# A two-layer GELU block on one core: the last wait of the program moves from SyncE to GpSimd

## The chip, the core and the metric

The kernel runs on one core of a Trainium2 chip. The metric is the device time of one execution in microseconds (us). A core has five engines with instruction streams of their own: TensorE (PE, matrix multiplication; its weight loads are listed as PEld), VectorE (DVE), ScalarE (ACT), GpSimd (POOL) and SyncE (SP), which only issues transfers and waits. The engines meet through semaphores alone: an instruction or a transfer raises one when it is done, and another engine waits until it has a given value. A transfer raises its semaphore by 16 when all of its data has landed.

## The reference

```python
B, S, D, F = 1, 2048, 448, 1792          # bfloat16 throughout

def reference(x, w1, b1, w2, b2):
    h = jnp.einsum("bsd,df->bsf", x, w1) + b1
    h = _gelu(h)                          # the tanh approximation
    return jnp.einsum("bsf,fd->bsd", h, w2) + b2
```

## The kernel before

**Tiles and stages.** The 2048 tokens are worked on in four chunks of 512 (`NSC`), the 1792 hidden features in fourteen tiles of 128 (`NFT`). TensorE first turns the first chunk of x with matmuls against an identity matrix (`turn_x`); the other three chunks come in turned by the transfers. The first layer (`l1`, matmuls at L275) runs over all pairs of chunk and feature tile, in an order that is written out by hand for the opening, while the weights are still arriving. ScalarE applies bias and GELU to each finished PSUM bank (L380) and writes `g_sb`. The second layer (`l2`, matmuls at L354) goes over the sixteen token tiles of 128, fourteen matmuls each. VectorE adds the second bias (L408) and writes `out_sb`.

**Outputs.** The list `outs` has seventeen entries: fifteen token tiles of 448 columns, and the last token tile cut in two, 320 columns and 128 columns. VectorE raises `sem_osb` by one after each. Every store is made by the helper `store` (L173) and raises `sem_od` by 16 when it has landed.

**Who issues and who waits.** SP (`sync_work`, from L217) issues nearly all loads and then the first sixteen stores, each behind a wait for its `sem_osb`. ScalarE (`scalar_work`) issues two loads at its start and the last store, of 128 columns, at its end. GpSimd (`gpsimd_work`) builds the identity matrix (a memset at L235 and an affine_select at L237), issues one small load (L242) that fills up rows of `b1n_sb`, and ends. The last instruction of `sync_work`, at L232, is the wait for all seventeen stores: `sem_od` at 16 x 17 = 272. No other engine waits for `sem_od`. At the start of the program all five engines pass a barrier (listed at L432), in which GpSimd gathers the others and releases them.

Of the kernel before, what the change touches and what calls it, by code (L numbers as in the profile page):

```python
# [11 lines left out]
def bass_standalone__dense_activation_gelu__prompt_kernel(  # L12
# [105 lines left out]
    outs = [(j, 0, D) for j in range(NST - 1)] + [(NST - 1, 0, OCUT), (NST - 1, OCUT, D)]  # L118
# [6 lines left out]
    with ExitStack() as es:  # L125
# [38 lines left out]
        sem_od = S_("sem_od")  # L164
# [5 lines left out]
        def store(eng, n):  # L170
            j, c0, c1 = outs[n]
            to = out0_view[:, j, c0:c1] if j < STC else out2[j * P:(j + 1) * P, c0:c1]
            eng.dma_start(to, out_sb[:, j, c0:c1]).then_inc(sem_od, 16)  # L173
# [7 lines left out]
        def load_w1p(eng, k, i):  # L181
            a, b = W1_PIECES[i]
            r = KROW[k]
            with nc.allow_non_contiguous_dma(reason="w1 column pieces"):
                eng.dma_start(
                    w1_sb[:, k, a * P:b * P], w1[r:r + P, a * P:b * P]
                ).then_inc(sem_w1p[k][i], 16)

        def load_w1(eng):
            with nc.allow_non_contiguous_dma(reason="w1 column pieces"):  # L190
                for k in (3, 2):
                    n, r = ROWS[k], KROW[k]
                    eng.dma_start(w1_sb[0:n, k, 0:WCUT], w1[r:r + n, 0:WCUT]).then_inc(sem_w1[k], 16)
                eng.dma_start(w1_sb[:, 3, WCUT:F], w1[KROW[3]:D, WCUT:F]).then_inc(sem_w13, 16)
                eng.dma_start(
                    w1_sb[:, 0:2, WCUT:F], w1[0:2 * P, WCUT:F].rearrange("(k p) f -> p k f", p=P)
                ).then_inc(sem_w1r, 16)
                eng.dma_start(
                    w1_sb[0:HALF, 2, WCUT:F], w1[KROW[2]:KROW[2] + HALF, WCUT:F]
                ).then_inc(sem_w1r, 16)  # L200

        def load_w2(eng, i):
            a, b = W2_PIECES[i]
            eng.dma_start(
                w2_sb[:, a:b, :], w2[a * P:b * P, :].rearrange("(ft p) d -> p ft d", p=P)
            ).then_inc(sem_w2[i], 16)

        def load_xT(eng, c):
            for k, d0 in enumerate(KROW):
                eng.dma_start(  # L210
                    xT_sb[:, k, c * SC:(c + 1) * SC],
                    x2[c * SC:(c + 1) * SC, d0:d0 + P],
                    transpose=True,
                ).then_inc(sem_x[c], 16)

        def sync_work(sp):
            sp.dma_start(xn_sb[:, 0:2, :], x0_view[:, 0:2, :]).then_inc(sem_xn[0], 16)  # L217
            sp.dma_start(xn_sb[:, 2:4, :], x0_view[:, 2:4, :]).then_inc(sem_xn[1], 16)
            load_w1p(sp, 0, 1)
            for i in range(len(W1_PIECES)):  # L220
                load_w1p(sp, 1, i)
            load_w1(sp)
            load_xT(sp, 1)
            for c in range(2, NSC):
                load_xT(sp, c)
            for i in range(len(W2_PIECES)):
                load_w2(sp, i)
            sp.dma_start(b2_bc[:, :], b2.partition_broadcast(P)).then_inc(sem_b2, 16)
            for n in range(len(outs) - 1):
                sp.wait_ge(sem_osb, n + 1)  # L230
                store(sp, n)
            sp.wait_ge(sem_od, 16 * len(outs))  # L232

        def gpsimd_work(pool):
            pool.memset(ident[:, :], 0.0).then_inc(sem_id, 1)  # L235
            pool.wait_ge(sem_id, 1)
            pool.affine_select(  # L237
                out=ident[:, :], in_=ident[:, :], compare_op=ALU.not_equal, fill=1.0,
                base=0, pattern=[[-1, P]], channel_multiplier=1,
            ).then_inc(sem_id, 1)  # L240

            pool.dma_start(b1n_sb[NFT:SQ, :], w1[0:SQ - NFT, 0:P]).then_inc(sem_b1x, 16)  # L242

        def tensor_work(pe):
            ones_w = nc.const_aps.tensor(1.0, [P, P], BF16)
# [166 lines left out]


        sync_work(nc.sync)
        gpsimd_work(nc.gpsimd)
        tensor_work(nc.tensor)
        scalar_work(nc.scalar)
# [29 lines left out]
```

## Time and profile before

| what | value |
|---|---|
| median of three runs | 93.5 us (93.33 to 93.71) |
| the profiled execution | 93.2 us |
| its span, from the program's first instruction to the end of its last | 91.9 us |
| granted TensorE clock, mean over the span | 1.00 |
| TensorE busy | 89.2 us |
| ScalarE busy | 36.6 us |
| VectorE busy | 12.8 us |
| GpSimd busy | 1.3 us, 7 instructions |
| stores, from issue to landing | 1.5 to 2.6 us, median 1.7 us |

The span holds only the program's own instructions. The execution's time is longer than the span by what lies before the first and after the last of them, and the trace has no row for that part. Semaphore instructions and the issue of transfers are not counted as busy; they stand in the rows of the queues (SPq, ACTq, POOLq). "L173" is line 173 of the kernel; a line of a helper such as `store` collects the instructions of all who call it.

### The profile page before, as it was taken

How to read it: one execution, taken by the hardware profiler on the slowest of the kernel's cores; microseconds unless marked ns; L12 is line 12 of the kernel's file. 1: busy time of each engine (PE TensorE's matmuls, PEld its weight loads, DVE VectorE, ACT ScalarE, POOL GpSimd, SP SyncE). 2: the span in 40 equal slices, each digit the busy share in tenths (PEclk: the TensorE clock that was granted, in tenths of full speed). 3: DMA queues.
4: the chain of work that ended last, by engine and by line, in shares of the span. 5: the costliest groups of instructions: out<-in, count | busy, mean ns of one | idle time of the engine just before them, and what ended most of it. 6: DMA issues, size and time to landing. Idle time of an engine off the chain costs nothing.

```text
span 91.9 us, 1491 instructions
## 1 busy us (share of the span) xinstructions
PE 89.2 (97%) x650; PEld 47.3 (52%) x650; DVE 12.8 (14%) x27; ACT 36.6 (40%) x61; POOL 1.3 (1%) x7
## 2 busy tenths in 40 slices
PE   6999999999999999999999999999999999999991
PEld 4664445555555555555545555555555555555571
DVE  0172000000000000000000122222112222221141
ACT  2640999877977788778974000000000000000000
POOL 5000000000000000000000000000000000000000
PEclk9999999999999999999999999999999999999999
DMA  1999856445795000000000111011111100111111
GB/s 26 342 303 274 143 112 85 95 101 114 199 375 182 0 0 4 7 0 0 0 0 0 50 55 47 7 48 50 50 50 50 50 28 29 50 50 50 50 50 50
DMA packets 12594, 7.29 MB, mean 79 GB/s; under 512 B 7203, under 2 KB 12396, under 8 KB 12588
## 3 DMA queue, kind: packets, MB, share of 16 engines
q1 hardware_dynamic: 12240, 7.03, 29.1%
q10 hardware_dynamic: 316, 0.17, 0.6%
q8 instruction: 5, 0.08, 0.3%
q0 software_dynamic: 32, 0.00, 0.0%
q14 instruction: 1, 0.01, 0.0%
HBM read 3.79 MB, written 1.84 MB: 61 GB/s over the span
## 4 chain that ended last, share of the span: by engine, by line
PE 97%; DVE 0%; issue 0%
PE ps L275 46%; PE ps L354 46%; PE ps L248 3%; PE ps L258 2%; DVE out_sb L408 0%
## 5 line engine op out<-in xcount | busy, mean ns | idle before, releaser
L275 PE MATMUL ps<-xT_sb,wi_sb 64*128 64x512 bf16 (+2 forms) x384 | 42.8, 374 | 0.0
L354 PE MATMUL ps<-wo_sb,g_sb 128*128 128x448 bf16 (+2 forms) x238 | 42.6, 342 | 0.0
L380 ACT ACTIVATE g_sb<-ps,bi_f 128x512 bf16<-128x512 f32 x56 | 33.7, 694 | 9.5 <-PE ps L275 9.5
L354 PEld LDWEIGHTS ps<-wo_sb,g_sb 128*128 128x128 bf16 x238 | 22.7, 98 | 20.2 <-issue 0.4
L275 PEld LDWEIGHTS ps<-xT_sb,wi_sb 64*128 64x128 bf16 (+1 forms) x384 | 21.8, 94 | 20.4 <-issue 0.7
L408 DVE TENSOR_TENSOR out_sb<-ps,bo_bc 128x448 bf16<-128x448 f32 (+2 forms) x17 | 10.2, 597 | 71.2 <-PE ps L354 71.2
L248 PE MATMUL ps<-const-bfloat16-1.0 128*128 128x256 bf16 x12 | 2.7, 417 | 0.8 <-PEq L432 0.8
L248 PEld LDWEIGHTS ps<-const-bfloat16-1.0 128*128 128x128 bf16 x12 | 1.6, 143 | 1.4 <-issue 0.8
L372 ACT ACT_TABLE_LOAD x1 | 1.3, 1283 | 1.8 <-issue 1.8
L376 ACT CAST xT_sb<-ps 128x512 bf16<-128x512 f32 (+1 forms) x3 | 1.5, 514 | 1.3 <-PE ps L258 1.3
L391 DVE CAST xT_sb<-ps 128x256 bf16<-128x256 f32 x3 | 1.2, 422 | 4.2 <-PE ps L258 4.2
L258 PE MATMUL ps<-ident,xn_sb 128*128 128x128 bf16 x16 | 1.6, 251 | 0.0
L258 PEld LDWEIGHTS ps<-ident,xn_sb 128*128 128x128 bf16 x16 | 1.3, 116 | 0.6 <-issue 0.5
L404 DVE COPY wi_sb<-wi_sb 64x512 bf16<-64x512 bf16 (+1 forms) x2 | 0.6, 286 | 2.0 <-DMA wi_sb<-in_w_dram 2.0
L396 DVE STREAM_TRANSPOSE bit_sb<-bin_sb 32x32 bf16<-32x32 bf16 x4 | 0.8, 200 | 0.1
L242 POOL DMA_DIRECT2D bin_sb<-in_w_dram x1 | 0.7, 655 | 0.2 <-issue 0.2
L237 POOL TENSOR_SCALAR_AFFINE_SELECT ident<-ident 128x128 bf16<-128x128 bf16 x1 | 0.3, 287 | 0.2 <-POOL ident L235 0.2
L372 ACT ACTIVATE act_junk<-const-float32-0.0 128x8 bf16<-128x8 f32 x1 | 0.2, 208 | 0.0
L235 POOL MEMSET ident<- 128x128 bf16 x1 | 0.2, 204 | 0.3 <-POOLq L432 0.3
L398 DVE CAST bi_f<-bit_sb 128x14 f32<-128x14 bf16 x1 | 0.2, 175 | 0.0
L432 POOL MEMSET const-float32-0.0<- 128x1 f32 x1 | 0.1, 98 | 0.2 <-issue 0.2
L432 POOL MEMSET const-bfloat16-1.0<- 128x1 bf16 x1 | 0.1, 101 | 0.0
(2 smaller groups left out, 0.2 us busy)
## 6 DMA issues: line engine op xcount, KB each, us to landing
out_dram<-out_sb SPq DMA_DIRECT2D x15, 112.0 KB, 1.7
wo_sb<-in_w_dram SPq DMA_DIRECT2D x2, 784.0 KB, 5.5
wi_sb<-in_w_dram SPq DMA_DIRECT2D x4, 128.0 KB, 3.5
xn_sb<-in_x_dram SPq DMA_DIRECT2D x2, 224.0 KB, 2.8
wi_sb<-in_w_dram SPq DMA_DIRECT2D x1, 384.0 KB, 5.1
wi_sb<-in_w_dram SPq DMA_DIRECT2D x1, 256.0 KB, 4.0
wi_sb<-in_w_dram SPq DMA_DIRECT2D x1, 192.0 KB, 4.5
xT_sb<-in_x_dram SPq DMA_TRANSPOSE x12, 3.4
```

What stands on the lines that cost most here:

```text
L242: pool.dma_start(b1n_sb[NFT:SQ, :], w1[0:SQ - NFT, 0:P]).then_inc(sem_b1x, 16)
L248: pe.matmul(ps[0][:, 0:WN], lhsT=ones_w, rhs=ones_x, start=True, stop=True)
L258: mm = pe.matmul(ps[XBANK[n]][:, col:col + P], lhsT=xn_sb[:, 2 * h + t, KROW[k]:KROW[k] + P], rhs=ident[:, :], start=True, stop=True,)
L275: return pe.matmul(bank("g", i)[:, t0:t1], lhsT=w1_sb[lo:hi, k, ft * P:(ft + 1) * P], rhs=xT_sb[lo:hi, k, c * SC + t0:c * SC + t1], start= ...
L354: mm = pe.matmul(bank("o", n)[:, 0:c1 - c0], lhsT=g_sb[:, ft, j * P:(j + 1) * P], rhs=w2_sb[:, ft, c0:c1], start=(ft == 0), stop=(ft == NF ...
L372: act.activation(act_junk[:, :], zero, ACT.Gelu_apprx_tanh)
L376: act.copy(*x_part(n, parts)).then_inc(sem_xTa, 1)
L380: act.activation(g_sb[:, ft, c * SC:(c + 1) * SC], bank("g", i)[:, :], ACT.Gelu_apprx_tanh, bias=b1_f[:, ft:ft + 1], scale=1.0,).then_inc( ...
L391: dve.tensor_copy(*x_part(n, parts)).then_inc(sem_xTd, 1)
L396: dve.transpose(b1t_sb[to, :], b1n_sb[:, to]).then_inc(sem_b1T, 1)
L404: dve.tensor_copy(two(HALF, 2), two(0, 3)).then_inc(sem_dup, 1)
L408: dve.tensor_tensor(out=out_sb[:, j, c0:c1], in0=bank("o", n)[:, 0:c1 - c0], in1=b2_bc[:, c0:c1], op=ALU.add,).then_inc(sem_osb, 1)
```

## The change

The wait for all stores is taken out of SP's stream and put at the end of GpSimd's. SP's last instruction is then its sixteenth store; GpSimd's last instruction is the wait. The semaphore and the count are the same.

```diff
@@ -229,7 +229,6 @@
             for n in range(len(outs) - 1):
                 sp.wait_ge(sem_osb, n + 1)
                 store(sp, n)
-            sp.wait_ge(sem_od, 16 * len(outs))
 
         def gpsimd_work(pool):
             pool.memset(ident[:, :], 0.0).then_inc(sem_id, 1)
@@ -240,6 +239,7 @@
             ).then_inc(sem_id, 1)
 
             pool.dma_start(b1n_sb[NFT:SQ, :], w1[0:SQ - NFT, 0:P]).then_inc(sem_b1x, 16)
+            pool.wait_ge(sem_od, 16 * len(outs))
 
         def tensor_work(pe):
```

## The prediction, made before the changed kernel had run

> **What bounds the kernel now.** I read the page's busy times first, then the chain that ended last in order of time, then the timeline of the last microseconds, then what SP's queue waited for, and last the start of the program, because it is the only place where GpSimd (POOL) and SP do the same thing side by side.
>
> The head of the page and its busy times:
>
> ```profile
> span 91.9 us, 1491 instructions
> PE 89.2 (97%) x650; PEld 47.3 (52%) x650; DVE 12.8 (14%) x27; ACT 36.6 (40%) x61; POOL 1.3 (1%) x7
> ```
>
> TensorE is busy for 89.2 of 91.9 us; GpSimd runs seven instructions. The chain that ended last (start us, length us, what):
>
> ```profile
> 5.48 42.02 PE ps L275 x380
> 47.49 42.53 PE ps L354 x238
> 90.02 0.02 issue
> 90.05 0.29 DVE out_sb L408
> ```
>
> The chain is TensorE from 0.8 to 90.0 us and one VectorE addition. It stops at 90.34 us (90.05 + 0.29), because the chain follows work and not transfers; the span ends 1.56 us later. The timeline from 85 us on shows what fills that:
>
> ```profile
> 89.26 0.49 DVE L408 TENSOR_TENSOR out_sb<-ps,bo_bc 128x320 bf16<-128x320 f32 x1 [1.28 <-PE ps L354]
> 90.05 0.29 DVE L408 TENSOR_TENSOR out_sb<-ps,bo_bc 128x128 bf16<-128x128 f32 x1 [0.29 <-PE ps L354]
> 90.37 0.35 ACTq L173 DMA_DIRECT2D out_dram<-out_sb  x1
> ```
>
> ScalarE's queue issues the last store at 90.37 us, 0.03 us after the addition. The DMA part of the page gives 1.5 us from that issue to landing, so it lands at about 91.87 us. SP's queue waits for it:
>
> ```profile
> SPq L173 <- DVE out_sb L408: 60.8, 16, 27.3
> SPq L232 <- DMA out_dram<-out_sb: 1.7, 1, 1.7
> L232 SPq EVENT_SEMAPHORE  x1: 17/17/17, 91.9 to 91.9; - x1
> ```
>
> The first two lines are SP's waits (us in total, times, longest); the third is the record of line 232 (duration in ns, then its start). SP is done with its sixteen stores at 90.1 us, waits 1.7 us, and its wait record of 17 ns closes the span. So the tail is: last addition, ScalarE's issue, landing, and whoever stands at that wait.
>
> **The change, part by part.** The profiled execution took 93.2 us, which is its span of 91.9 us and 1.3 us that lie outside the program's own instructions. The median of the three runs is 93.5 us, so I add 0.3 us to any sum made against the profiled execution.
>
> *Removed:* one 17 ns record on SP at 91.875 us (91.892 less 0.017). SP then ends with the store of outs[15]; its issue starts at 89.78 us by the trace and lasts 0.33 us, so SP ends at 90.1 us. Nothing stands behind line 232 on SP, and nothing waits for it.
>
> *Added:* one wait on POOL for the same semaphore with the same count, 16 x 17 = 272. It opens with the same landing at 91.87 us. POOL's records of this kind, at the start of the program, have the same length as SP's:
>
> ```profile
> L432 POOLq EVENT_SEMAPHORE  x2: 17/17/17, 0.5 to 0.6; - x2
> L432 SPq DRAIN  x1: 7/7/7, 0.0 to 0.0; - x1
> L432 POOLq DRAIN  x1: 193/193/193, 0.3 to 0.3; - x1
> L432 SPq EVENT_SEMAPHORE  x1: 17/17/17, 0.7 to 0.7; - x1
> ```
>
> 17 ns against 17 ns: the exchange of the record itself is worth 0.00 us. In program order the wait stands after POOL's memset, its affine_select and its one DMA issue (L242, 1.66 to 2.32 us), so none of them moves, and nothing is queued behind it. From 2.32 us on POOL has no work in either version, and nobody waits for POOL after the identity and the b1x load are there. The wait passes no issue on POOL's queue, and SP's queue issues the same 16 stores at the same times. The cover of all this is POOL's idleness; if POOL had to issue anything after 2.32 us, that issue would stand behind the wait until 91.87 us, but there is no such instruction. TensorE's 89.2 us, the last addition and ScalarE's issue are untouched, so the landing at 91.87 us stays.
>
> *How late POOL notices.* No row shows POOL waiting for a DMA. From below: when POOL and SP leave the opening barrier together, POOL's first instruction starts at 0.74 us and SP's first issue at 0.75 us, so POOL is no slower at leaving a wait, within 0.01 us. From above: between POOL's memset (ends 0.94 us) and the affine_select that waits for its semaphore (starts 1.18 us) lie 0.23 us, against 0.03 us between VectorE's addition and ScalarE's issue. That larger figure includes the end of the memset's writes and a register instruction, which a bare wait does not have. So 0.0 to +0.2 us; I take 0.0, because the barrier row is a sequencer's wait as this one is.
>
> *What follows the last wait.* The 1.3 us outside the span is the only part of the time that is large enough to matter, and the trace has no instruction in it. How it divides between the front and the end is not shown. If all of it is what SP has to do after its last instruction, and POOL needs nothing, the change gains 1.3 us. If POOL needs twice as long as SP, as its DMA issue does (655 ns at L242 against 332 ns for SP's stores), the change loses 1.3 us. So -1.3 to +1.3 us. The nearest rows are again at the start: the engines' first records begin at 0.0 us for SP, 0.1 us for VectorE, ScalarE and POOL, and 0.3 us for TensorE. The core is thus entered at SP first and POOL comes 0.1 us behind. If it is left through the same order, with SP nearest to the exit, an end that is reported by POOL instead of SP has about 0.1 us more to go. I take +0.1 us, as this is the only row that tells the two engines apart at a program boundary.
>
> [...]
>
> Sum against the profiled execution: 93.2 + 0.0 (record) + 0.0 (noticing) + 0.1 (leaving) = 93.3 us; with the 0.3 us to the median, **93.6 us**. About 0.5%, or 0.47 us, is what a measurement of this kernel can tell from no change, and 0.1 us is far inside it.
>
> **The rivals.**
>
> *SP's ending is the long one (faster).* If each engine does closing work of its own when its stream ends, SP's starts at 91.89 us today and is fully exposed, while POOL's is over since shortly after 2.32 us. With the change SP's closing starts at 90.1 us, 1.8 us before the end, and even 1.3 us of it would be hidden. Next in line would be ScalarE, whose stream ends at 90.72 us (90.37 + 0.35); with 1.3 us of its own it would be through at 92.0 us, 0.1 us after POOL's wait opens. The gain is the difference between SP's closing and POOL's: half of 1.3 us gives 92.9 us, all of it 92.2 us. For it: SP issues 41 of the 44 transfers that it and ScalarE issue, so if there is queue state to put in order, SP has most. Against it: the rows at the start show no longer step on SP than on POOL. It decides from a difference of 0.47 us on. Chance 0.25.
>
> *POOL's ending is the long one (slower).* The same mechanism with the sign turned: POOL's closing work is hidden behind some 89 us of idleness now and would begin only at 91.89 us. It decides where POOL needs over 0.47 us more than SP. [...] Against it: the long drain stands behind four memsets that it waits for, and POOL's only DMA landed 3.5 us after its issue, so nothing of it is open at the end. Half of the bound gives 93.5 + 0.65 = 94.2 us, the whole 94.8 us. Chance 0.32.
>
> *The move does not reach the measured time.* If the measured time ends with the last transfer or with something that all engines share, the wait's place is without effect: 93.5 us. This is inside the forecast's band and shares its chance. That the wait on POOL would open early can be left aside: the count of 272 needs all seventeen stores.
>
> **How the numbers follow.** Forecast within 0.5% (93.03 to 93.97 us): 0.43, likeliest value 93.6 us. Faster by over 0.5%: 0.25, spread over 92.2 to 93.0 us. Slower by over 0.5%: 0.32, spread over 94.0 to 94.8 us. I leave POOL's ending the larger of the two outer chances because more rows are longer on POOL than on SP. For a range that holds 8 in 10 I cut about a third of each outer case: 92.5 to 94.5 us. The band of the forecast alone is 93.2 (0.2 us of noise and 0.1 us of a shorter ending below 93.5) to 93.9 us (0.1 us, 0.2 us of late noticing and 0.1 us of noise above it).
>
> **What the changed profile would show.** The wait's record should stand on POOL's queue at line 242 or just after it, 17 ns long, starting within 0.2 us of the landing of ScalarE's last store, and the list of SP's waits should have L173 alone. The last addition should end at about 90.3 us and the span stay at 91.9 us; TensorE's busy time should stay at 89.2 us. The difference between the profiled execution and its span, 1.3 us now, is where the rivals are decided: 1.3 to 1.4 us would bear out the forecast, under 0.9 us the faster rival, over 1.7 us the slower one. I would be wrong in another way if the span itself moved by more than 0.2 us: POOL would then notice the landing later than any row here lets me expect, or the stores would land at another time.

## The result and the profile after

The changed kernel takes 94.22 us (median of nine runs, 93.83 to 94.62), against 93.65 us for the kernel before (nine runs, 93.33 to 94.00). The ratio is 1.0077, with a 95% interval of 1.0050 to 1.0104: slower by about 0.7 us, between 0.5 and 1.0 us (the two medians differ by 0.57 us). The profiled execution took 94.53 us.

The head of the page of the changed kernel, and its costliest group in the first layer's opening (line, engine, operation, tiles, count | busy us, mean ns | idle before):

```profile
span 92.7 us, 1491 instructions
PE 90.0 (97%) x650; PEld 48.2 (52%) x650; DVE 12.8 (14%) x27; ACT 36.8 (40%) x61; POOL 1.4 (1%) x7
...
L258 PE MATMUL ps<-ident,xn_sb 128*128 128x128 bf16 x16 | 2.1, 308 | 0.0
```

The chain that ended last (start us, length us, what) has the same links as before:

```profile
3.50 1.39 PE ps L258 x12
4.89 0.85 PE ps L275 x4
5.74 0.43 PE ps L258 x4
6.17 42.10 PE ps L275 x380
48.27 42.53 PE ps L354 x238
90.80 0.02 issue
90.82 0.29 DVE out_sb L408
```

The span of this execution is 0.8 us longer than that of the one shown for before, and all of it is there by 6.17 us, where the long run of L275 begins (5.48 us before). From there on the chain is the same length: 42.1 and 42.5 us. So nothing in it comes from the end of the program. The nine executions of the changed kernel have spans from 92.0 to 92.8 us, with a median of 92.3; the profiled one is among the longest. Before's median of 93.65 us less the 1.31 us outside its span gives 92.34 us, the same, and 58 executions of before that ran beside the experiments have spans from 91.7 to 93.0 us, with a median of 92.3. A long opening is thus a thing of single executions, and it is taken up in the last section.

The end of the span, by the timeline and by the record of the moved wait (duration in ns, first and last start in us):

```profile
90.82 0.29 DVE L408 TENSOR_TENSOR out_sb<-ps,bo_bc 128x128 bf16<-128x128 f32 x1 [0.29 <-PE ps L354]
91.15 0.36 ACTq L173 DMA_DIRECT2D out_dram<-out_sb  x1
```

```profile
L242 POOLq EVENT_SEMAPHORE  x1: 17/17/17, 92.7 to 92.7; - x1
```

The wait stands on GpSimd's queue, 17 ns long. From the start of ScalarE's issue to the start of the wait's record there are 1.518 us (91.147 to 92.665 us in the trace); before it was 1.507 us (90.368 to 91.875). GpSimd notices the landing as early as SP did, within 0.011 us. SP's list of waits has lost line 232:

```profile
SPq L173 <- DVE out_sb L408: 60.9, 16, 27.4
SPq L432 <- PEq L432: 0.7, 1, 0.7
```

What is left is the part of the time that no row of these views shows. The profiled execution of before took 93.20 us with a span of 91.892 us: 1.31 us outside. That of the changed kernel took 94.53 us with a span of 92.682 us: 1.85 us outside. All nine executions of the changed kernel have 1.81 to 1.93 us outside (their spans are given to 0.1 us), while their spans move by 0.8 us; the 58 executions of before have 1.26 to 1.39 us. So the change costs 0.54 us after the last instruction of the program: 93.65 + 0.54 = 94.19 us, against the measured 94.22 us, and 0.54 of 93.65 us is 0.58%, inside the interval.

### The profile page after: what moved, and what is told of

Its sections match the earlier page's. It is cut to its first block, busy times and chain, and to the rows that moved or that the text cites. A ratio compares the mean times of both kernels' runs of the same rounds, so it can differ in the third digit from the quotient of the medians.

```text
span 92.7 us, 1491 instructions
## 1 busy us (share of the span) xinstructions
PE 90.0 (97%) x650; PEld 48.2 (52%) x650; DVE 12.8 (14%) x27; ACT 36.8 (40%) x61; POOL 1.4 (1%) x7
## 3 DMA queue, kind: packets, MB, share of 16 engines
HBM read 3.79 MB, written 1.84 MB: 61 GB/s over the span
## 4 chain that ended last, share of the span: by engine, by line
PE 97%; DVE 0%; issue 0%
PE ps L275 46%; PE ps L354 46%; PE ps L248 3%; PE ps L258 2%; DVE out_sb L408 0%
## 5 line engine op out<-in xcount | busy, mean ns | idle before, releaser
L275 PE MATMUL ps<-xT_sb,wi_sb 64*128 64x512 bf16 (+2 forms) x384 | 43.4, 376 | 0.0
L275 PEld LDWEIGHTS ps<-xT_sb,wi_sb 64*128 64x128 bf16 (+1 forms) x384 | 22.2, 95 | 20.3 <-issue 0.7
L258 PE MATMUL ps<-ident,xn_sb 128*128 128x128 bf16 x16 | 2.1, 308 | 0.0
L258 PEld LDWEIGHTS ps<-ident,xn_sb 128*128 128x128 bf16 x16 | 1.7, 142 | 0.5 <-issue 0.4
```

The costliest lines, as they stand in the source:

```text
L258: mm = pe.matmul(ps[XBANK[n]][:, col:col + P], lhsT=xn_sb[:, 2 * h + t, KROW[k]:KROW[k] + P], rhs=ident[:, :], start=True, stop=True,)
L275: return pe.matmul(bank("g", i)[:, t0:t1], lhsT=w1_sb[lo:hi, k, ft * P:(ft + 1) * P], rhs=xT_sb[lo:hi, k, c * SC + t0:c * SC + t1], start= ...
```

## The experiments

The time outside the span proved far steadier than the time itself, so each kernel was judged by it first. In the third column it is the time of the profiled execution less its span in the trace's nanoseconds; in the fourth it is the median of all executions and their range, from spans that are given to 0.1 us. The 58 executions of before are those that ran beside e1 to e4 (27) and beside e5, e10, e7 and e8 (31).

| kernel | who has the last wait | outside, us | outside, all executions | time, ratio to before (95%) |
|---|---|---|---|---|
| before | SP | 1.31 | 1.31 (1.26 to 1.39), 58 | 1 |
| changed | GpSimd | 1.85 | 1.84 (1.81 to 1.93), 9 | 1.0077 (1.0050 to 1.0104) |
| e1_both | SP and GpSimd | 1.85 | 1.84 (1.81 to 1.91), 6 | 1.0091 (1.0056 to 1.0127) |
| e2_act | ScalarE | 1.45 | 1.47 (1.42 to 1.49), 10 | 0.9987 (0.9961 to 1.0013) |
| e3_dve | VectorE | 1.43 | 1.40 (1.37 to 1.47), 10 | 1.0001 (0.9971 to 1.0032) |
| e4_pe | TensorE | 1.59 | 1.58 (1.52 to 1.63), 10 | 1.0028 (1.0001 to 1.0056) |
| e5_pool_noq | GpSimd, no transfer of its own | 1.85 | 1.84 (1.81 to 1.91), 10 | 1.0073 (1.0036 to 1.0110) |
| e10_nosel | GpSimd, no affine_select | 1.84 | 1.86 (1.83 to 1.91), 10 | 1.0033 (0.9994 to 1.0072) |
| e11_idle | GpSimd, nothing else to do | 1.85 | one execution | no interval |
| e6_sp_noq | SP, GpSimd without a transfer | 1.33 | one execution | no interval |
| e7_pool_osb | SP; GpSimd waits to 1.5 us before | 1.32 | 1.31 (1.26 to 1.39), 10 | 1.0036 (1.0006 to 1.0066) |
| e8_pool_16 | SP; GpSimd waits to 0.5 us before | 1.39 | 1.38 (1.35 to 1.41), 10 | 1.0046 (1.0013 to 1.0079) |

### Is it GpSimd's late end or SP's early one? (e1_both)

```diff
             pool.dma_start(b1n_sb[NFT:SQ, :], w1[0:SQ - NFT, 0:P]).then_inc(sem_b1x, 16)
+            pool.wait_ge(sem_od, 16 * len(outs))
```

SP's wait stays where it was.

> SP keeps its last wait and GpSimd gets the same one behind its load. In the changed kernel the time outside the span is 1.8 to 1.9 us against 1.3 us before. Theory A (what GpSimd has to do after its stream is about 0.55 us longer than what SP has to do, and starts only when its wait opens): outside 1.85 us, time 0.55 us above before, because GpSimd again leaves last. Theory C (it is SP's early end that costs): SP ends as late as before, so outside 1.3 us and no change.

1.85 us outside, and 94.59 us against 93.65 us. That is 0.94 us more, and the time outside accounts for 0.54 us of it; the rest lies in the spans, whose median is 92.75 us in these six executions against 92.3 us in the 27 of before. The records of the two waits in this kernel (by their lines):

```profile
L232 SPq EVENT_SEMAPHORE  x1: 17/17/17, 92.7 to 92.7; - x1
```

```profile
L243 POOLq EVENT_SEMAPHORE  x1: 17/17/17, 92.7 to 92.7; - x1
```

They start 6 ns apart (92.736 us on SP, 92.742 us on GpSimd), so both engines let go of the same landing at the same time, and the execution still ends as late as with GpSimd alone. SP's early end is without effect (theory C falls), and so is the noticing.

### The other engines (e2_act, e3_dve, e4_pe)

In each of the three SP's wait is taken out and stands at the end of another engine's stream:

```diff
-            sp.wait_ge(sem_od, 16 * len(outs))
...
             store(act, len(outs) - 1)
+            act.wait_ge(sem_od, 16 * len(outs))
```

```diff
                 ).then_inc(sem_osb, 1)
+            dve.wait_ge(sem_od, 16 * len(outs))
```

```diff
             for c in range(NSC):
                 l2(c)
+            pe.wait_ge(sem_od, 16 * len(outs))
```

> SP's last wait goes to ScalarE, behind its own last store; GpSimd ends at 2.3 us as before. Theory A: outside the span stands ScalarE's own ending, a new number that need not lie near GpSimd's; by the opening rows, where ScalarE's drain and wait are as short as SP's, 1.3 to 1.5 us. Theory B (the ending is passed on from engine to engine, and the cost is the distance from SP in the order in which the engines' first records begin: SP 0.00, VectorE 0.12, ScalarE 0.13, GpSimd 0.14, TensorE 0.32 us): about 1.8 us, as for GpSimd. Theory C: 1.85 us, as SP ends early here too.

> SP's last wait goes to VectorE, behind its last addition. Theory A: VectorE's own ending, 1.3 to 1.5 us outside the span if it follows the opening rows. Theory B: about 1.75 us, a little under GpSimd. Theory C: 1.85 us.

> SP's last wait goes to TensorE, behind its last matmul. Theory A: TensorE's own ending; its opening wait record is 51 ns against 17 ns for SP, so if the ending consists of such records it could be up to three times SP's, 1.3 to 3.9 us outside the span. Theory B: the farthest from SP in the opening order, so over 2 us outside. Theory C: 1.85 us.

The records of the wait, of the kernels with ScalarE, VectorE and TensorE in this order:

```profile
L385 ACTq EVENT_SEMAPHORE  x1: 17/17/17, 92.1 to 92.1; - x1
```

```profile
L411 DVEq EVENT_SEMAPHORE  x1: 21/21/21, 92.1 to 92.1; - x1
```

```profile
L366 PEldq EVENT_SEMAPHORE  x1: 51/51/51, 92.6 to 92.6; - x1
```

Outside stand 1.45, 1.43 and 1.59 us. SP ends early in all three, so theory C falls a second time. Each engine has a number of its own, as theory A says, with SP's 1.31 us the smallest. Theory B, one price per step of distance from SP, fails in size: it wanted about 1.8 us for ScalarE and VectorE, which begin no more than 0.02 us ahead of GpSimd, and over 2 us for TensorE. Something is left of it all the same. The extra over SP is 0.13 us for VectorE, 0.15 for ScalarE and 0.28 for TensorE; their first records in before begin 0.12, 0.13 and 0.32 us after SP's. By that row GpSimd should have cost 0.14 us, and it costs 0.40 us more. What the extras are made of shows in the changes of semaphores after the span, further down.

The times agree with this only as far as they can. For VectorE and TensorE the extra of 0.13 and 0.28 us is 0.14% and 0.30%, inside the intervals; for ScalarE it is 0.16%, just above the upper end of 0.13%.

### What makes GpSimd's ending long? (e5_pool_noq, e10_nosel, e11_idle, e6_sp_noq)

The first takes GpSimd's only transfer away (ScalarE issues it), the second its affine_select, both with the wait on GpSimd:

```diff
-            pool.dma_start(b1n_sb[NFT:SQ, :], w1[0:SQ - NFT, 0:P]).then_inc(sem_b1x, 16)
...
             load_w1p(act, 0, 0)
+            act.dma_start(b1n_sb[NFT:SQ, :], w1[0:SQ - NFT, 0:P]).then_inc(sem_b1x, 16)
```

```diff
-            pool.memset(ident[:, :], 0.0).then_inc(sem_id, 1)
-            pool.wait_ge(sem_id, 1)
-            pool.affine_select(...).then_inc(sem_id, 1)
+            pool.memset(ident[:, 0:HALF], 0.0).then_inc(sem_id, 1)
+            pool.memset(ident[:, HALF:P], 0.0).then_inc(sem_id, 1)
```

> The changed kernel, but the small load for the b1 rows is issued by ScalarE, so GpSimd issues no transfer at all and its last wait stands behind the affine_select. Outside the span: 1.31 us before, 1.85 us in the changed kernel. Theory P1 (GpSimd's ending is longer because it has its own transfer queue to put in order): 1.3 to 1.5 us outside, time within 0.2 us of before. Theory P2 (it is the configuration that the affine_select loads) and P3 (it is fixed for this engine, whatever it ran): 1.85 us outside, time as in the changed kernel.

> The changed kernel without the affine_select: two memsets of half the identity tile take its place, so x is turned against zeros and that part of the computation is left out. GpSimd still issues its load. Theory P2: 1.3 to 1.5 us outside the span. Theories P1 and P3: 1.85 us.

1.85 and 1.84 us. Neither the transfer (P1) nor the affine_select (P2) matters by itself. Then both were taken away together, with the two memsets moved to VectorE, and as a control the transfer was moved while SP kept the wait:

> The changed kernel with nothing of the kernel's own left on GpSimd but the last wait: ScalarE issues the small load, and VectorE writes the identity tile with two memsets of zeros, so x is turned against zeros and that part of the computation is left out. Theory P3 (GpSimd's longer ending is fixed for this engine): 1.85 us outside the span. If the affine_select and the load each were enough to cause it, so that taking away either alone showed nothing: 1.3 to 1.5 us.

> The control to the run without a transfer on GpSimd: the small load on ScalarE, the last wait on SP as before. Theory A: 1.31 us outside the span, since SP leaves last. A value of 1.85 us here would say that the load's move, and not the waiting engine, sets the time outside.

All that GpSimd still runs ahead of its wait in the first of them is what the program's opening puts there (timeline: start us, length us, engine, line):

```profile
0.24 0.10 POOL L427 MEMSET const-float32-0.0<- 128x1 f32 x1 [0.24 <-issue]
0.27 0.10 POOL L427 MEMSET const-float32-1.0<- 128x1 f32 x1
0.30 0.10 POOL L427 MEMSET const-bfloat16-1.0<- 128x1 bf16 x1
0.33 0.10 POOL L427 MEMSET const-uint8-127<- 128x1 uint8 x1
```

1.85 us outside, and 1.33 us in the control. Whatever GpSimd has to do at the end does not depend on what this kernel gave it to do: P3 stands. Whether those four memsets or the other records of the opening are its cause was not tried; every kernel here has them.

### Is it covered when GpSimd ends earlier? (e7_pool_osb, e8_pool_16)

```diff
             pool.dma_start(b1n_sb[NFT:SQ, :], w1[0:SQ - NFT, 0:P]).then_inc(sem_b1x, 16)
+            pool.wait_ge(sem_osb, len(outs))
```

```diff
+        sem_ol = S_("sem_ol")
...
-            eng.dma_start(to, out_sb[:, j, c0:c1]).then_inc(sem_od, 16)
+            eng.dma_start(to, out_sb[:, j, c0:c1]).then_inc(sem_od if n < len(outs) - 1 else sem_ol, 16)
...
-            sp.wait_ge(sem_od, 16 * len(outs))
+            sp.wait_ge(sem_od, 16 * (len(outs) - 1))
+            sp.wait_ge(sem_ol, 16)
...
+            pool.wait_ge(sem_od, 16 * (len(outs) - 1))
```

> SP keeps its wait for all stores; GpSimd gets a wait at the end of its stream for the last addition (17 in sem_osb), which opens some 1.5 us before SP's. Theory A (the endings run beside each other, each from its own engine's last instruction): GpSimd's ending is over 1.5 + 1.31 - 1.85 = 0.97 us before SP's, so 1.31 us outside the span and no change of time. Theory D (a long last wait on GpSimd costs 0.54 us in itself, wherever it opens): 1.85 us outside, time 0.54 us over before.

> The last store gets a semaphore of its own. GpSimd waits for the sixteen stores of SP alone, SP for those and the last one. By the trace of before, store 16 is issued at 89.78 us and lands 1.6 us later, so GpSimd's wait opens at about 91.4 us and SP's at 91.9 us. Theory A: GpSimd is through at 91.4 + 0.02 + 1.85 = 93.27 us and SP at 91.89 + 1.31 = 93.20 us, so the 0.54 us is covered but for some 0.1 us: 1.31 to 1.45 us outside. Theory D: 1.85 us.

The records of the two waits, first of the kernel where GpSimd waits for the last addition, then of the one where it waits for sixteen stores:

```profile
L243 POOLq EVENT_SEMAPHORE  x1: 17/17/17, 91.1 to 91.1; - x1
```

```profile
L232 SPq EVENT_SEMAPHORE  x1: 17/17/17, 92.6 to 92.6; - x1
```

```profile
L245 POOLq EVENT_SEMAPHORE  x1: 17/17/17, 92.3 to 92.3; - x1
```

```profile
L234 SPq EVENT_SEMAPHORE  x1: 28/28/28, 92.8 to 92.8; - x1
```

With 1.51 us of lead (91.141 against 92.648 us) the outside is 1.32 us, SP's own value, though GpSimd waits nearly as long as in the changed kernel. Theory D falls: a long last wait is not dear, a late one is. With a lead of 0.48 us (92.291 against 92.768) it is 1.39 us. GpSimd's record ends at 92.308 us there; adding its 1.85 us gives 94.16 us, SP's 92.796 us and 1.31 us give 94.10 us, and the execution ended at 94.19 us. The later of the two sums holds within 0.03 us.

The times of these two kernels are higher than before's all the same, by 0.24 and 0.47 us in the medians (93.87 and 94.10 us against 93.63 us), with both intervals above 1. The spans hold that difference: their medians are 92.5 and 92.75 us, against 92.3 us in the 31 executions of before beside them, while the time outside is 1.31 and 1.38 us against 1.32 us. So no change of time, as theory A had it, is borne out for the end of the program and not for the whole. Whether a wait on GpSimd lengthens spans is not shown: over the six such kernels with several executions the median span runs from 91.95 us (e10) to 92.75 us (e1, e8), over the four without one from 92.1 to 92.5 us.

**What follows the span.** No row of the views lies behind the span, but the traces also keep the changes of semaphores, and these go on. Semaphore 2, which no instruction of the kernel names, is raised nine times in a chain that ends as the program's first record begins (0.37 us long in before and in the changed kernel). It is raised nine times again at the program's end, then some 230 to 250 changes of other semaphores pass within 0.6 to 0.7 us, and then come nine more steps, which take 0.36 us in every trace. Times in the table are us from the end of the span; "made before" are the steps of the first closing chain that were made by then.

| last wait | kernel | steps made before | next step | chain done | last change of all | outside |
|---|---|---|---|---|---|---|
| SP | before | 4 | 0.13 | 0.29 | 1.44 | 1.31 |
| VectorE | e3_dve | 3 | 0.14 | 0.38 | 1.56 | 1.43 |
| ScalarE | e2_act | 1 | 0.11 | 0.43 | 1.58 | 1.45 |
| TensorE | e4_pe | 0 | 0.19 | 0.55 | 1.72 | 1.59 |
| GpSimd | changed | 2 | 0.55 | 0.83 | 1.97 | 1.85 |
| SP, GpSimd 0.48 us earlier | e8_pool_16 | 2 | 0.06 | 0.34 | 1.52 | 1.39 |

The last change comes 0.11 to 0.14 us beyond the time outside in all twelve traces, so the differences arise here, at the end, and not ahead of the program. From the end of the first chain to the last change there are 1.15 to 1.18 us, whoever waits. What differs is the first chain. By the counts in the table its first steps belong to TensorE, ScalarE, GpSimd, VectorE and SP, in this order. It stands still where the step of the late engine is due, and from that step to its end it takes 0.16 us for SP and 0.28 us for GpSimd. And GpSimd needs 0.55 us from the end of its wait to its step, where the others need 0.11 to 0.19 us. So its 0.54 us over SP are 0.12 us for its place in the chain and 0.42 us of a delay of its own. From wait to step it takes the same 0.54 to 0.55 us in e5, e10 and e11, and in e8 it takes them from GpSimd's own earlier wait on (92.308 to 92.854 us). What GpSimd does in that time no record shows.

None of these kernels is better than the kernel before: SP has the shortest ending of the five engines, 1.31 us against 1.43 to 1.85 us.

## Why the prediction was right and wrong

**What held.** The record exchange was worth nothing: 17 ns for 17 ns. Noticing was taken as 0.0 us out of a bound of 0.0 to 0.2: 6 ns between SP and GpSimd on one landing. The links of the chain and the 1.5 us from the last issue to the wait stayed, GpSimd's wait stood at line 242, and nothing was queued behind it. The whole effect sits where the text put all of its doubt, in the time outside the span, and the mark it gave for the slower rival, a difference of over 1.7 us, was passed at 1.85 us. The measured 94.22 us lies in the stated range and in that rival's stretch of 94.0 to 94.8 us. The range held because it was wide enough to take in that rival; the forecast's own sum did not reach so far.

**What failed.** The likeliest value, 93.6 us, and its own band up to 93.9 us. The step that failed is the last term of the sum, the leaving, taken as +0.1 us; it measured 0.54 us. GpSimd's place in the closing chain is 0.12 us of that, close to what the term allowed; the delay of 0.42 us that GpSimd has for itself had no place in the sum. The term was read off the order in which the engines' first records begin, and that row was good for three engines and wrong by 0.40 us for the fourth, the one in question. The slower rival had the right mechanism, with the price of 0.54 us near its half-bound of 0.65 us. That nearness is luck, since no row stood behind taking half of the 1.3 us. The rival was held back by two remarks, that GpSimd's long opening drain only waits for memsets and that its one transfer is long over. Both looked for the cost in what the kernel gives GpSimd, and e5, e10 and e11 show that it is not there. GpSimd's longer steps in before, a drain of 193 ns against 7 ns for SP and an issue of 655 against 332 ns, were right in direction only: its transfer issue played no part (1.85 us outside without it, in e5).

Three signs failed for another reason. The span was to stay at 91.9 us, TensorE's busy time at 89.2 us and the end of the last addition at 90.3 us; the profiled execution has 92.7, 90.0 and 91.1 us. The text took one execution's span for the kernel's, while before's own spans run from 91.7 to 93.0 us. So its warning that a span moved by more than 0.2 us would mean a late notice or a late landing does not hold either.

**The faster rival** had the right form, an ending of each engine's own that is hidden if the engine ends early: in e7 and e8 GpSimd's hides (1.32 and 1.39 us outside), as the text said SP's would. It failed on which engine has the long one. What is hidden is only an engine's way to its step in the closing chain; the rest, from the end of that chain on, took 1.15 to 1.18 us whoever ended early.

**The early end of SP** bought nothing: with it 1.43 to 1.85 us stand outside (the changed kernel and e2 to e4), and with SP held to the end beside GpSimd 1.85 us as well (e1). The changes of semaphores show what the execution waits for: the first closing chain stands still until the late engine's step, with four steps made before the span's end where SP is late and none where TensorE is. The place in the chain is worth 0.12 of the measured 0.54 us between SP and GpSimd, and GpSimd's own delay 0.42 us. What GpSimd does in its extra time stays open: the trace has no instruction there.

## What to carry to other kernels

In this kernel the program's last wait has a price that depends on the engine that makes it, in time that lies outside the span, where no row shows it: 1.31 us on SP, 1.43 to 1.59 us on VectorE, ScalarE and TensorE, 1.85 us on GpSimd. Leave the last wait to SP, and let GpSimd end more than half a microsecond earlier: with a lead of 1.51 us its longer ending was covered, with 0.48 us all but 0.06 to 0.09 us of it. When a change at the end of a program is judged, compare time less span execution by execution: over 58 executions of before it stayed within 0.13 us, rounding of the spans included, while the span itself moved by 1.3 us.

## What the runs showed that was not expected

Spans of one kernel differ by more than the change costs, and the difference comes from the first half of the program. In all twelve profiled executions the first matmul of the second layer starts between 47.25 and 48.32 us, and from there to the end of the span it is 44.47 to 44.51 us. Most of it arises in the opening. In the profiled execution of before, the matmuls of L258 start 107 ns apart at 3.9 us and 55 ns apart from 4.4 us on; in that of the changed kernel they keep 107 ns until 5.9 us, and the first of L275 that follow at 109 ns apart begin at 6.2 us. TensorE had been busy since 0.79 us in both. The mean per matmul shows it in the groups of line 258 (257 in the kernel with ScalarE's wait), of before, of the kernel with ScalarE's wait and, further up, of the changed one (308 ns):

```profile
L258 PE MATMUL ps<-ident,xn_sb 128*128 128x128 bf16 x16 | 1.6, 251 | 0.0
```

```profile
L257 PE MATMUL ps<-ident,xn_sb 128*128 128x128 bf16 x16 | 1.7, 276 | 0.0
```

The granted clock reads 1.00 in all of them, so that column doesn't show this. Six of the traces hold a record of the granted clock, and it starts at the step: full clock from 4.12 us in before and from 4.60 us in the kernel with ScalarE's wait. The changed kernel's trace has no such record.

Over the twelve profiled executions the step came between 3.80 us (e3) and about 6.4 us (e8), the earliest 3.0 us after TensorE's first matmul. What sets its moment is not shown. As it lies at such different times, and nine spans of the changed kernel and 58 of before have the same median of 92.3 us, the long opening of the one profiled execution says nothing about the change.
